# The second product of two token groups with the tokens moving instead of the weights, the gate applied to its inputs, and a dozen smaller moves

## The chip, the cores and the metric

One core of a Trainium2 chip runs the whole program. Its engines work side by side, each through its own queue in order: TensorE (PE in the profile, its weight loads PEld), VectorE (DVE), ScalarE (ACT), GpSimd (POOL) and SyncE (SP), which only issues DMAs here. The metric is device time in microseconds, the median of several runs.

## The reference, cut to what matters

```
# 4 batches, 8 heads, 576 positions, head 64: windowed attention, window 64
x = softmax(mask(q @ k.T / 8)) @ v           -> x [2304, 512]
x = elu(x @ w_in) @ w_out                    # w_in [512, 2048]
logits = x @ w_gate                          # [2304, 8]
P = exp(logits - max); 8 times: rows to sum 1, columns to sum 2304/8
out = sum over e of P[:, e] * (relu(x @ w1[e]) @ w2[e])    # 8 experts, w1[e] [512, 1024]
```

All of it is float32. Every product is made of three fp32r products (high x high, high x low, low x high), so each operand is split into a rounded high part (ScalarE) and a remainder (VectorE or GpSimd).

## The kernel before

The order of the work is written out by hand: the functions append instructions to each engine's queue in the order in which the loops at the end call them, and no scheduler reorders them.

Attention (0 to about 185 us) goes through pairs of heads: `pair_load` and `v_load` fetch q, k, v, `pair_T` transposes q and k on TensorE (L316), `grp_S`, `grp_E`, `grp_N`, `grp_P`, `grp_V` make scores, exponentials, normalisation, transposes and the product with v. `v_shift` makes a copy of v that is shifted by 64 rows. `warm` puts matmuls with zeros between. The loads stand on SP's queue.

The first feed-forward block (to about 520 us) has steps of `step_in` and `step_out` (L204 to 206, L531 to 533), four 128-wide slices of w_in at a time over five blocks of tokens (four of 512, one of 256); `elu` hands its later parts on through `run_later`.

The gate is interleaved with the last of these steps and the first expert steps: `gate_a` computes the logits of a block with the eight experts (and their low halves) on the partitions, `gate_b` turns them round with small matmuls against `sel` (L576), and `sink_parts` does the row and column normalisations on `Pr`, one piece per expert step.

The experts come in two ways. For the first 768 tokens and experts 0 to 4 they are plain (`e_in`, `e_out`, to about 866 us), while VectorE, ScalarE and GpSimd also prepare the sums of weight blocks (`p_tasks`, `q_tasks`) that the second way needs and SP stores them.

From 866 us on the second way runs: a seven-product (Winograd form of Strassen) scheme over groups g of 768 tokens, group 0 with experts 5 to 7, groups 1 and 2 with all eight. A period is one group, one expert and half of its hidden columns; there are 6 + 16 + 16 = 38 of them, each of seven steps. A step has two calls of `l1` (six matmuls each, 128x128 weights standing, 384 tokens moving, L1046) and one call of `l2` for a period that began eight steps earlier (18 matmuls, L1119: 128 tokens of the hidden layer standing, 256 columns of w2 moving). In `l1` the running sums in PSUM are copied out by ScalarE (`keep`, L1059; L1081 for `r21`) or added by VectorE (`add`, L1054; L1076), sums are made on VectorE (`ssum`, L1063), and `hid` and `hid_low` split them into high (ScalarE, L1019) and low part (VectorE L1024, GpSimd L1028). TensorE may add the next product to such a running sum only when the copy of the last one is done. `l2` adds its three 128x256 results to the accumulator `oa[g]` with the gate `Pr` as a scalar per token (VectorE, L1140; L1138 the first time), and in the last period of a group the finished quarter is stored. All groups share one accumulator buffer, so that a group's first L1138 waits for the store of the group before.

Of the kernel before, what the change touches and what calls it, by code (L numbers as in the profile page):

```python
# [18 lines left out]
def kernel(  # L19
# [14 lines left out]
    nc = tc.nc  # L34
# [30 lines left out]
    sel = const.tile([2 * E, E], F32, name="sel")  # L65
# [191 lines left out]
    def pair_load(pi):  # L257
# [3 lines left out]
        for z, (nm, src) in enumerate((("q", q), ("k", k))):  # L261
# [279 lines left out]
    def moe1_out(st, extra):  # L541
        step_out(st)
        u, j, i = st
        if u == NU - 1 and i == UF - 1:
# [7 lines left out]
            if j == len(blocks) - 2:  # L552
                extra += sink_parts()
# [4 lines left out]
    def gate_a(j):  # L558
# [7 lines left out]
        t = work.tile([P, TB], F32, tag="m", bufs=2, name="lgT")[:2 * E]  # L566
        nc.vector.tensor_copy(t[:, :n], lg[:2 * E, :n])
        lgT[j] = t

    def gate_b(j):  # L570
        t0, n = blocks[j]
        lt = ps_sm("lt")
        nt = n // P
        t = lgT.pop(j)
# [4 lines left out]
        nc.vector.tensor_copy(  # L579
            Lg[:, t0 // P:t0 // P + nt, :], lt[:, :nt * E].rearrange("p (t e) -> p t e", e=E)  # L580
        )
# [3 lines left out]
    def sink_parts():  # L585
# [35 lines left out]
        def cols():  # L621
# [3 lines left out]
            nc.vector.tensor_scalar(rc, t[:, :E], 1e-9, None, op0=ALU.add)  # L625
            nc.vector.reciprocal(rc, rc)
            nc.vector.tensor_scalar(rc, rc, float(NT) / E, None, op0=ALU.mult)
# [12 lines left out]
        return [p0, p1, first] + [mid] * 7 + [cols]  # L640
# [273 lines left out]

    P2 = {}
# [95 lines left out]

    chains = {}
# [20 lines left out]
    def l1(k, n, p, pi):  # L1033
# [17 lines left out]

        def add(nm, a):
            t = tmp("c", 5, nm)
            nc.vector.tensor_tensor(out=t, in0=o, in1=d[a], op=ALU.add)  # L1054
            d[nm] = t
# [8 lines left out]

        if pi == 1:
            keep("a")
        elif pi == 2:
            add("c11", "a")
            hid_low(*hid(key, 0, d["c11"], True))
        elif pi == 6:  # L1070
            keep("u")
        elif pi == 5:
# [3 lines left out]
            nc.vector.tensor_tensor(out=t, in0=c, in1=d["v"], op=ALU.add)  # L1076
            d["c22"] = t
            hid_low(*hid(key, 2, t, True))
        elif pi == 3:
            d["r21"] = tmp("s", 6, "r21")  # L1080
            nc.scalar.activation(d["r21"], o, AF.Relu)  # L1081
            ssum("s3", "c11", "r21", ALU.subtract)
            h3 = hid(key, 5, d["s3"], False)
            ssum("s1", "c22", "r21", ALU.add)
            ssum("s2", "c11", "s1", ALU.subtract)
            h2 = hid(key, 4, d["s2"], False)
            h1 = hid(key, 3, d["s1"], False)
            for h in (h3, h2, h1):
                hid_low(*h)
        elif pi == 4:  # L1090
            add("c21", "u")
            h1 = hid(key, 1, d["c21"], True)
            ssum("s4", "c21", "s2", ALU.add)
            hid_low(*h1)
            after.append(lambda: hid_low(*hid(key, 6, d["s4"], False)))
            del chains[key]


# [3 lines left out]
    def l2(k, x):  # L1102
        g, e, pp = periods[k]
        pi = out_order[x]
        if x == 0:
            banks.reverse()
            ot["A"] = P2["ps2"].tile([P, 1024], F32, tag=banks[0], bufs=1, name=banks[0])
            if k and periods[k - 1][0] != g:
# [6 lines left out]
        fresh = pi in (1, 7, 2)  # L1115
        for c in range(3):
# [10 lines left out]
        i, j, init = {  # L1127
            1: (0, 0, True), 7: (1, 1, True), 6: (1, 0, True), 4: (1, 0, False),
            5: (1, 1, False), 2: (0, 0, False), 3: (0, 1, True),
        }[pi]  # L1130
        last = pi in (2, 5, 4, 3)
# [9 lines left out]
        if last and e == E - 1 and pp == NP // 2 - 1:  # L1141
# [7 lines left out]
    with tc.manual_schedule():  # L1149
# [26 lines left out]
        for n in range(2):  # L1176
            pair_T(n)
            warm(2)
# [34 lines left out]
        for m in range(NST + 3):  # L1213
# [26 lines left out]
            for n in old:  # L1240
                if n > NG and n % NG == 0:
# [16 lines left out]
            for n in new:  # L1258
                if n and n % NG == 0:
# [14 lines left out]
        nc.vector.tensor_copy(sel[0:E, :], ident[0:E, 0:E])  # L1274
        nc.sync.dma_start(out=sel[E:2 * E, :], in_=ident[0:E, 0:E])
# [25 lines left out]
        for s, st in enumerate(steps):  # L1301
# [5 lines left out]
            if s:  # L1307
# [107 lines left out]
        for nm in ("w2p", "hp", "tp"):  # L1415
# [68 lines left out]
```

## Time and profile before

| | |
|---|---|
| three runs | 2008.22, 2011.4, 2015.02 us, median 2011.4 |
| profiled execution | 2014.06 us, span of its instructions 2011.6 us |
| TensorE busy | 1989.5 us, 99% of the span |
| VectorE, ScalarE, GpSimd busy | 69%, 43%, 38% |
| granted clock | mean 0.998 |

The page's engine rows count an engine as busy while an instruction of it runs, and matmuls overlap, so a busy TensorE can still lose time between two starts. The number that matters is from the start of one run of matmuls to the start of the next.

### The profile page before, as it was taken

What the parts mean: (1) busy time and instruction counts of PE and PEld (TensorE: products, weight loads), DVE (VectorE), ACT (ScalarE), POOL (GpSimd) and SP (SyncE); (2) the same over time, 40 slices, a digit from 0 to 9 for tenths busy, and PEclk for the clock granted to TensorE, in tenths of its full rate; (3) what the DMA queues carried; (4) which work ended last, traced back from release to release, by engine and by line L of the source; (5) the groups of instructions that cost most, each with busy time, mean ns of one, the idle gap of its engine ahead of it and who ended that gap; (6) DMA issues with size and microseconds to landing.
All of it is one profiled execution on the core that took longest, in us unless ns stands there. A gap on an engine that the chain in (4) does not pass through costs nothing.

```text
span 2011.6 us, 36449 instructions
## 1 busy us (share of the span) xinstructions
PE 1989.5 (99%) x13190; PEld 1844.9 (92%) x13190; DVE 1394.1 (69%) x2727; ACT 860.6 (43%) x1839; POOL 755.7 (38%) x725
## 2 busy tenths in 40 slices
PE   9999999999999999999999999999999999999998
PEld 7778888898888888889999999999999999999998
DVE  6745676767698665657776776767777767777676
ACT  8766455555443443333343333333333333333332
POOL 5323232334255555343363332332344323333332
PEclk9999999999999999999999999999999999999999
DMA  9751254458599999958878878778788788887784
GB/s 212 160 106 40 76 177 155 164 187 294 203 364 337 369 364 367 333 196 270 277 247 270 250 250 247 252 250 248 247 276 274 247 245 250 250 250 248 249 247 128
DMA packets 290866, 481.59 MB, mean 239 GB/s; under 512 B 78528, under 2 KB 145152, under 8 KB 286848
## 3 DMA queue, kind: packets, MB, share of 16 engines
q1 hardware_dynamic: 290608, 479.24, 74.7%
q8 instruction: 105, 1.72, 0.3%
q14 instruction: 73, 0.60, 0.1%
q10 hardware_dynamic: 80, 0.03, 0.0%
HBM read 348.14 MB, written 126.88 MB: 236 GB/s over the span
## 4 chain that ended last, share of the span: by engine, by line
PE 83%; DVE 5%; issue 4%; DMA 3%; ACT 3%; POOL 1%; SPq 1%; DVEq 0%; POOLq 0%; ACTq 0%
PE la L1046 15%; PE oa L1119 13%; PE ob L1119 13%; PE lb L1046 11%; PE ac L884 2%; PE ac L883 2%; PE ac L885 2%; PE p L867 2%; PE p L866 2%; PE p L865 2%; PE p L205 2%; PE p L206 2%; PE p L204 2%; PE ac L532 2%; PE ac L533 2%
## 5 line engine op out<-in xcount | busy, mean ns | idle before, releaser
L1028 POOL TENSOR_TENSOR h<-s,h 128x384 fp32r<-128x384 f32 x304 | 373.4, 1246 | 714.4 <-ACT h L1019 506.6
L1046 PE MATMUL la<-xf,w1f 128*128 128x384 f32 x1824 | 363.1, 337 | 6.8 <-ACT u L1059 6.2
L1046 PEld LDWEIGHTS la<-xf,w1f 128*128 128x128 f32 x1824 | 312.6, 189 | 9.8 <-ACT u L1059 8.6
L1119 PE MATMUL oa<-w2f,h 128*128 128x256 f32 x2394 | 307.3, 282 | 0.8 <-DVE acc L1140 0.8
L1119 PE MATMUL ob<-w2f,h 128*128 128x256 f32 x2394 | 307.2, 282 | 0.0
L1119 PEld LDWEIGHTS oa<-w2f,h 128*128 128x128 f32 x2394 | 302.0, 190 | 1.0 <-DVE acc L1140 1.0
L1119 PEld LDWEIGHTS ob<-w2f,h 128*128 128x128 f32 x2394 | 302.0, 190 | 0.0
L1024 DVE SCALAR_TENSOR_TENSOR h<-c,h 128x384 fp32r<-128x384 f32 x228 | 194.2, 852 | 129.9 <-ACT h L1019 120.9
L1046 PE MATMUL lb<-xf,w1f 128*128 128x384 f32 x1368 | 275.1, 335 | 0.2 <-DVE c L1076 0.2
L1046 PEld LDWEIGHTS lb<-xf,w1f 128*128 128x128 f32 x1368 | 237.7, 189 | 0.7 <-DVE c L1076 0.7
L1019 ACT ACTIVATE h<-s 128x384 fp32r<-128x384 f32 x304 | 150.7, 519 | 181.2 <-DVE s L1063 101.4
L1140 DVE SCALAR_TENSOR_TENSOR acc<-oa,Pr,acc 128x256 f32<-128x256 f32 x393 | 165.2, 475 | 43.1 <-PE oa L1119 43.1
L1019 ACT ACTIVATE h<-c 128x384 fp32r<-128x384 f32 x228 | 117.8, 517 | 171.7 <-DVE c L1054 113.4
L1140 DVE SCALAR_TENSOR_TENSOR acc<-ob,Pr,acc 128x256 f32<-128x256 f32 x381 | 160.2, 475 | 38.3 <-PE ob L1119 38.3
L704 POOL TENSOR_TENSOR sw<-rw 128x256 f32<-128x256 f32 x110 | 103.8, 943 | 208.5 <-DVE f L734 158.1
L246 ACT ACTIVATE hh<-p 128x512 fp32r<-128x512 f32 (+1 forms) x80 | 39.3, 491 | 196.7 <-PE p L867 196.7
L1059 ACT ACTIVATE v<-la 128x384 f32<-128x384 f32 x76 | 37.4, 492 | 198.2 <-PE la L1046 198.2
L1063 DVE SCALAR_TENSOR_TENSOR s<-c,s 128x384 f32<-128x384 f32 x152 | 98.1, 646 | 16.1 <-DVE s L1063 0.5
L865 PE MATMUL p<-xh,f 128*128 128x512 f32 (+1 forms) x320 | 108.6, 339 | 0.0
L867 PE MATMUL p<-xh,f 128*128 128x512 f32 (+1 forms) x320 | 107.6, 336 | 0.0
L866 PE MATMUL p<-xl,f 128*128 128x512 f32 (+1 forms) x320 | 107.5, 336 | 0.0
L247 DVE SCALAR_TENSOR_TENSOR hl<-p,hh 128x512 fp32r<-128x512 f32 (+1 forms) x80 | 44.3, 556 | 89.7 <-ACT hh L246 89.7
(159 smaller groups left out, 3639.6 us busy)
## 6 DMA issues: line engine op xcount, KB each, us to landing
w1f<-wdi SPq DMA_DIRECT2D x532, 256.0 KB, 3.8
w2f<-wdo SPq DMA_DIRECT2D x266, 512.0 KB, 4.1
wdo<-f SPq DMA_DIRECT2D x28, 1024.0 KB, 7.4
rw<-in_moe_w_dram SPq DMA_DIRECT2D x220, 128.0 KB, 4.4
wdi<-f SPq DMA_DIRECT2D x27, 1024.0 KB, 6.8
wdo<-f SPq DMA_DIRECT2D x28, 768.0 KB, 5.3
wdi<-f SPq DMA_DIRECT2D x27, 768.0 KB, 5.0
raw<-in_moe_w_in_dram SPq DMA_DIRECT2D x16, 512.0 KB, 4.4
```

The source lines that it names most:

```text
L247: nc.vector.scalar_tensor_tensor(gl[:, :n], p1[:, :n], 0.0, r(gh[:, :n]), op0=ALU.max, op1=ALU.subtract)
L704: nc.gpsimd.tensor_tensor(out=sw[:, o], in0=a, in1=b, op=op)
L865: nc.tensor.matmul(p1[:, :n], w[:, s, 0, cs], xh, start=(c == 0), stop=False)
L866: nc.tensor.matmul(p1[:, :n], w[:, s, 0, cs], xl, start=False, stop=False)
L867: nc.tensor.matmul(p1[:, :n], w[:, s, 1, cs], xh, start=False, stop=(c == NCC - 1))
L1019: nc.scalar.activation(h[:, 0], src, AF.Relu if relu else AF.Copy)
L1024: nc.vector.scalar_tensor_tensor(h[:, 1], src, 0.0, r(h[:, 0]), op0=ALU.max, op1=ALU.subtract)
L1028: nc.gpsimd.tensor_tensor(out=h[:, 1], in0=src, in1=r(h[:, 0]), op=ALU.subtract)
L1046: nc.tensor.matmul(o, w[:, a, c, :], x[:, b, c, :], start=first and c == 0 and z == 0, stop=last and c == 1 and z == 2, skip_group_check=True,
L1063: nc.vector.scalar_tensor_tensor(d[nm], d[a], 0.0, d[b], op0=ALU.max, op1=op)
L1119: nc.tensor.matmul(o[:, c * HB2:(c + 1) * HB2], hs[p][:, a, c * P:(c + 1) * P], w[:, p, b, :], start=fresh and c != 1 and p == 0 and z == ...
L1140: nc.vector.scalar_tensor_tensor(a, src, pe, a, op0=ALU.mult, op1=ALU.add)
```

## The change

- `l2` of groups 1 and 2 goes through a new `l2_flip`: a 128x128 piece of w2 stands and 384 tokens move, 12 matmuls in place of 18. The result has the output columns on the partitions, so the gate can no longer be a scalar per partition. Instead `scaled` multiplies c11, c22, c21 by a broadcast row of gate values (`pb`), and r21 is made with that multiplication on VectorE, where ScalarE made it before.
- `flip` writes `Pr` transposed to memory (`prd`), `pb_load` fetches it for an expert and group, repeated on all partitions.
- One VectorE addition of 128x768 drains a step (two of 128x384 for a finished quarter, a ScalarE copy for the first product), and `out_unit` transposes each finished 128x384 piece back on TensorE (three transposes, in a bank of `l1`'s tag lb), copies it on ScalarE and stores it. Group 2 takes over group 1's accumulator.
- `put` defers the splits of `l1` to `after`, which now runs behind the copies of the next `l1`. The first `l2` comes two steps earlier.
- The gate: `gate_a` transposes the logits on VectorE and adds the halves, `gate_b` brings them into place with four small DMAs; the sinkhorn pieces start one slot later, and one small VectorE instruction of each column pass goes.
- The start: k of the first pair is loaded on ScalarE's queue, four warming matmuls go, v of pair 2 is loaded and shifted one iteration earlier, and two `step_in` instead of one stand before the last block's `m0_out`.

```diff
@@ pair_load
-                nc.sync.dma_start(
+                (nc.scalar if pi == 0 and z else nc.sync).dma_start(
@@ moe1_out
-                extra += sink_parts()
+                extra += [lambda: None] + sink_parts()
@@ gate_a
-        nc.vector.tensor_copy(t[:, :n], lg[:2 * E, :n])
-        lgT[j] = t
+        nc.vector.transpose(t[:, :n], lg[:32, :n])
...
+        nc.vector.tensor_tensor(out=u..., in0=v[:, :, :, 0:E], in1=v[:, :, :, E:2 * E], op=ALU.add)
+        lgT[j] = u
@@ gate_b
-        for tt in range(nt):
-            nc.tensor.matmul(
-                lt[:, tt * E:(tt + 1) * E], t[:, tt * P:(tt + 1) * P], sel, start=True, stop=True
-            )
-        nc.vector.tensor_copy(Lg[...], lt[...])
+        for q in range(4):
+            nc.sync.dma_start(out=Lg[32 * q:32 * q + 32, t0 // P:(t0 + n) // P, :], in_=u[:, q])
@@ sink_parts
+        def flip():
...
+            nc.tensor.transpose(t[:, 0:P], f[:, 0:P], ident)
+            nc.tensor.transpose(t[:n, P:2 * P], f[:, P:], ident)
...
+            nc.sync.dma_start(out=prd[0:P], in_=st[:, 0:P])
+            nc.sync.dma_start(out=prd[P:P + n], in_=st[:n, P:2 * P])
-        return [p0, p1, first] + [mid] * 7 + [cols]
+        return [p0, p1, first] + [mid] * 7 + [cols, flip]
@@ new: pb_load
+        t = P2["pb"].tile([P, 2, TH], F32, tag="pb", bufs=2, name="pb")
+        src = prd.rearrange("(t e) p -> e t p", e=E)[e, 6 * g:6 * g + 6]
+        nc.sync.dma_start(out=t..., in_=src.partition_broadcast(P))
@@ l1
+        def scaled(t, i):
+            if g:
+                nc.vector.tensor_tensor(out=t, in0=t, in1=pb[g, e][:, i], op=ALU.mult)
+        def put(slot, nm, relu):
+            after.append(lambda: hid_low(*hid(key, slot, d[nm], relu)))
...
         elif pi == 2:
             add("c11", "a")
-            hid_low(*hid(key, 0, d["c11"], True))
+            put(0, "c11", True)
...
         elif pi == 3:
-            nc.scalar.activation(d["r21"], o, AF.Relu)
+            if g:
+                nc.vector.scalar_tensor_tensor(
+                    d["r21"], o, 0.0, pb[g, e][:, 1], op0=ALU.max, op1=ALU.mult
+                )
+            else:
+                nc.scalar.activation(d["r21"], o, AF.Relu)
@@ new: l2_flip and out_unit
+        for c in range(2):
+            for p in range(2):
+                for z, (a, b) in enumerate(((0, 0), (0, 1), (1, 0))):
+                    nc.tensor.matmul(o[:, c], w[:, p, b, c * P:(c + 1) * P], hs[p][:, a, :], ...)
+        for cs in ((0, 1), (1, 2)) if done else ((0, 2),):
...
+            if init:
+                nc.scalar.activation(a, src, AF.Copy)
+            else:
+                nc.vector.tensor_tensor(out=a, in0=src, in1=a, op=ALU.add)
+    def out_unit(g, acT, i, c):
+        o = P2["ps2"].tile([P, 512], F32, tag="lb", bufs=2, name="ot")
+        for t in range(TH // P):
+            nc.tensor.transpose(o[:, t * P:(t + 1) * P], acT[:, c, a:a + P], ident)
+        st = tmp("s", 6, "ost")
+        nc.scalar.activation(st, o[:, :TH], AF.Copy)
+        nc.sync.dma_start(out=out[...], in_=st...)
@@ l2
+            if g == 2:
+                oa[2] = oa[1]
@@ the loops
             pair_T(n)
-            warm(2)
-                    step_in(steps[0])
-                    queue.append(steps[0])
-                    run_later()
+                    for st in steps[:2]:
+                        step_in(st)
+                        queue.append(st)
+                        run_later()
+                        run_later()
...
+                    fs = list(after) if pi != 4 else []
+                    del after[:len(fs)]
                     l1(k, s * 2 + z, p, pi)
-                    if pi != 4:
-                        while after:
-                            after.pop(0)()
+                    for f in fs:
+                        f()
...
-            if s == LAG - 1:
+            if s == LAG - 3:
                 l2(0, 0)
```

## Rows read from the trace of the kernel before

**Rows 1.** The page's engine row, whole span: busy us, share, instructions.

```profile
PE 1989.5 (99%) x13190; PEld 1844.9 (92%) x13190; DVE 1394.1 (69%) x2727; ACT 860.6 (43%) x1839; POOL 755.7 (38%) x725
```

**Rows 2.** Waits of TensorE: who, for whom, us in total, times, longest.

```profile
PE la L1046 <- ACT u L1059: 6.2, 6, 2.5
...
PE pv L412 <- DMA ve<-vo: 1.9, 1, 1.9
PE p L485 <- DVE gl L235: 1.6, 2, 0.8
...
PE oa L1119 <- DVE acc L1140: 0.8, 1, 0.8
```

**Rows 3.** Chain of waits: start us, us, what.

```profile
953.34 2.08 PE la L1046 x12
955.42 2.15 PE oa L1119 x18
...
1072.29 4.57 DMA out_dram<-acc
```

**Rows 4.** Timeline of TensorE, start of the second way: start, us, instruction, idle before.

```profile
877.12 1.21 PE L1046 MATMUL lb<-xf,w1f 128*128 128x384 f32 x6
880.79 2.29 PE L1046 MATMUL la<-xf,w1f 128*128 128x384 f32 x6 [2.47 <-ACT u L1059]
...
889.68 0.52 PE L1119 MATMUL ob<-w2f,h 128*128 128x256 f32 x3
```

**Rows 5.** Timeline of ScalarE in the same stretch.

```profile
879.43 0.52 ACT L1019 ACTIVATE h<-c 128x384 fp32r<-128x384 f32 x1 [1.70 <-DVE c L1054]
...
880.27 0.47 ACT L1059 ACTIVATE u<-la 128x384 f32<-128x384 f32 x1
```

**Rows 6.** Windows: busy us (instructions) per engine; last granted clock, DMA share, GB/s.

```profile
882.00:884.00 2.00, 1.36 (x5) 0.85 (x4) 0.30 (x1) 0.49 (x1) 0.00 (x0) 0.50 0.55 211
...
1072.00:1990.00 918.00, 915.34 (x6480) 913.28 (x6479) 655.35 (x1273) 325.12 (x685) 315.46 (x254) 1.00 0.80 249
```

**Rows 7.** VectorE by line and form, whole span: count, busy us, mean ns.

```profile
L1140 DVE SCALAR_TENSOR_TENSOR acc<-oa,Pr,acc 128x256 f32<-128x256 f32 x393 | 165.2, 475 | 43.1 <-PE oa L1119 43.1
L1063 DVE SCALAR_TENSOR_TENSOR s<-c,s 128x384 f32<-128x384 f32 x152 | 98.1, 646 | 16.1 <-DVE s L1063 0.5
L1063 DVE SCALAR_TENSOR_TENSOR s<-c,r 128x384 f32<-128x384 f32 x152 | 78.0, 555 | 23.2 <-ACT r L1081 23.2
...
L1054 DVE TENSOR_TENSOR c<-lb,u 128x384 f32<-128x384 f32 x76 | 42.0, 552 | 0.0
...
L899 DVE TENSOR_TENSOR acc<-ac,acc 128x512 f32<-128x512 f32 x12 | 7.5, 677 | 0.0
...
L959 DVE TENSOR_TENSOR xb<-xb,xt 128x384 f32<-128x384 f32 x6 | 5.8, 984 | 0.0
```

**Rows 8.** Timeline of TensorE around one block's gate turn.

```profile
516.69 1.05 PE L576 MATMUL lt<-sel,lgT 16*128 16x8 f32 x8
517.67 0.50 PE L865 MATMUL p<-xh,f 128*128 128x512 f32 x1
```

**Rows 9.** Timeline of TensorE in attention, 40 to 53 us.

```profile
40.77 0.87 PE L397 MATMUL pt<-ident,sp 128*128 128x128 f32 x6
41.58 1.53 PE L348 MATMUL s<-qkT 64*64 64x128 f32 x24
...
52.26 0.33 PE L412 MATMUL pv<-pT,ve 64*64 64x64 f32 x4 [1.89 <-DMA ve<-vo]
```

**Rows 10.** Timeline of TensorE at the start.

```profile
5.79 0.55 PE L316 MATMUL ptr<-ident,kn 96*128 96x96 f32 x2 [0.23 <-DMA kn<-in_k_dram]
6.04 1.02 PE L1173 MATMUL warm<-gw 128*128 128x512 f32 x2
...
7.18 0.72 PE L1173 MATMUL warm<-gw 128*128 128x512 f32 x2
```

**Rows 11.** DMA issues: count, KB each, median us to landing.

```profile
out_dram<-acc SPq DMA_DIRECT2D x12, 384.0 KB, 3.3
```

More of the change, by code (lines that the diff above doesn't have):

```diff
@@ L64 @@
     mask = const.tile([P, P], F32, name="mask")
-    sel = const.tile([2 * E, E], F32, name="sel")
+    const.tile([P, E], F32, name="gap")
     gwr = const.tile([P, NCC, E], F32, name="gwr")
@@ L1093, in l1, with l2_flip @@
             ssum("s4", "c21", "s2", ALU.add)
-            hid_low(*h1)
-            after.append(lambda: hid_low(*hid(key, 6, d["s4"], False)))
+            put(1, "c21", True)
+            put(6, "s4", False)
             del chains[key]
+    units = []
+    def l2_flip(g, o, w, hs, fresh, i, j, init, done):
+        acT = oa[g].rearrange("p a d -> p (a d)").rearrange("p (c t) -> p c t", c=NCC)
+        o = o.rearrange("p (c n) -> p c n", c=2)[:, :, :TH]
+        for c in range(2):
+            for p in range(2):
+                for z, (a, b) in enumerate(((0, 0), (0, 1), (1, 0))):
+                    nc.tensor.matmul(
+                        o[:, c],
+                        w[:, p, b, c * P:(c + 1) * P],
+                        hs[p][:, a, :],
+                        start=fresh and p == 0 and z == 0,
+                        stop=False,
+                        skip_group_check=True,
+                    )
+        ts = slice(i * TH, (i + 1) * TH)
+        for cs in ((0, 1), (1, 2)) if done else ((0, 2),):
+            a = acT[:, 2 * j + cs[0]:2 * j + cs[1], ts]
+            src = o[:, cs[0]:cs[1]]
+            if init:
+                nc.scalar.activation(a, src, AF.Copy)
+            else:
+                nc.vector.tensor_tensor(out=a, in0=src, in1=a, op=ALU.add)
+        if done:
+            units.append([lambda c=c: out_unit(g, acT, i, 2 * j + c) for c in range(2)])
@@ L1107, in l2 @@
             ot["A"] = P2["ps2"].tile([P, 1024], F32, tag=banks[0], bufs=1, name=banks[0])
-            if k and periods[k - 1][0] != g:
+            if g == 2:
+                oa[2] = oa[1]
+            elif k and periods[k - 1][0] != g:
                 oa[g] = accp.tile([P, 6, DM], F32, tag="acc2", name="acc2")
@@ L1115, in l2 @@
         fresh = pi in (1, 7, 2)
+        i, j, init = {
+            1: (0, 0, True), 7: (1, 1, True), 6: (1, 0, True), 4: (1, 0, False),
+            5: (1, 1, False), 2: (0, 0, False), 3: (0, 1, True),
+        }[pi]
+        last = pi in (2, 5, 4, 3)
+        done = last and e == E - 1 and pp == NP // 2 - 1
+        if g:
+            l2_flip(g, o, w, hs, fresh, i, j, init and e == 0 and pp == 0, done)
+            return
         for c in range(3):
@@ L1140, in l2 @@
                 nc.vector.scalar_tensor_tensor(a, src, pe, a, op0=ALU.mult, op1=ALU.add)
-        if last and e == E - 1 and pp == NP // 2 - 1:
+        if done:
             t0 = (2 * g + i) * TH
@@ L1239 @@
                 pair_T(n)
-            for n in old:
-                if n > NG and n % NG == 0:
+            for n in mid if m == 4 else old:
+                if n > NG and n % NG == 0 and (n // NG > 2 or m == 4):
                     v_shift(n // NG)
@@ L1257 @@
             run_later()
-            for n in new:
-                if n and n % NG == 0:
+            for n in nxt if m == 2 else new:
+                if n and n % NG == 0 and (n // NG != 2 or m == 2):
                     v_load(n // NG)
@@ L1429 @@
                 after.pop(0)()
-            if s == LAG - 1:
+            fs = [f for u in units for f in u]
+            units.clear()
+            if s == LAG - 3:
                 l2(0, 0)
@@ L1436 @@
                 nw2 += 1
+            if j == 0 and k + 1 < NPD and periods[k + 1][0] and periods[k + 1][2] == 0:
+                pb_load(*periods[k + 1][:2])
             for k2 in (k, k + 1, k + 2):
@@ L1444 @@
                         close(xs["cm"])
+        for u in units:
+            for f in u:
+                f()
         close(ps2_cm)
-        for nm in ("tp", "hp", "w2p", "w1p", "xf"):
+        for nm in ("pb", "tp", "hp", "w2p", "w1p", "xf"):
             close(P2[nm + "_cm"])
```

67 lines of the change are left out of this document (43 added, 24 removed).

## The prediction

> **What bounds the kernel now.** The page's engine row comes first: TensorE is busy 1989.5 of 2011.6 us, no other engine over 69% [rows 1]. So the end moves only if TensorE gets less to issue, or stops waiting. What it issues is read from the chain of waits, in starts: in the second way a step is 12 matmuls with 384 tokens moving in 2.08 us, then 18 with 256 columns in 2.15 us [rows 3], 4.23 us together, and a period of seven steps 29.6 us. For what it waits, the list of waits is read: 6.2 us for the copies u of L1059, 1.9 us for a shifted v, 1.6 us for the last block's low parts, 0.8 us for a drain [rows 2]. The longest stands where the second way starts, and the timeline tells its price: after the six matmuls begun at 877.12, which take 1.04 us at the usual pace, five more sixes are through only at 889.68, so 11.5 us for 5.2 us of work, 6.3 us lost [rows 4]. Of these 2.47 us are the wait for u. ScalarE has u only at 880.27, behind two splits of which the first waits for VectorE [rows 5]. The windows show why the rest is lost too: after that wait the granted clock is 0.50, the 1.2 GHz level [rows 6].
>
> **The change, part by part.** The sum is made against the profiled execution, 2014.06 us, which is 2.7 us above the median of 2011.4; the end of it is shifted by that.
>
> *The flipped l2.* Groups 1 and 2 have 32 periods of seven, 224 calls. Each goes from 18 matmuls of 256 columns to 12 of 384, the same 4608 columns. `l1` issues exactly that shape, two 128-column pieces against 384 tokens, so its 2.08 us is the price: 0.07 us less a call, 15.7 us in all [rows 3]. If it saved nothing, 0; if the first matmul after a change of shape is what makes 2.15, up to that 15.7. I take 15.0.
> The Trainium skill ("TensorE: Matmul & The Clock Gate", Back-to-back issue gap) puts a warm matmul at N/2.4 + 2.5 ns. By it 18 x 109.2 becomes 12 x 162.5, 15 ns a call and 3.4 us in all. The trace disagrees: 2.15 us over 18 is 119 ns and 2.08 over 12 is 173 ns [rows 3], some 12 ns beyond the columns, not 2.5.
>
> *What VectorE gets for it.* Per period go seven times three drains at 475 ns, 10.0 us. In come seven drains of 128x768, which no row shows: from L1054 (384, 552 ns) to L899 (512, 677 ns) a column costs 0.98 ns, so 927 ns, 6.5 us; six gate multiplications, which lie between 555 and 984 ns by the nearest rows of two SBUF inputs, taken at 646, 3.9 us; two r21 at 552, 1.1 us [rows 7]. Net +1.5 us, on 655 us in 918, or 21.1 in a period of 29.6 [rows 6]: 22.6 of the new 29.1. It still fits, and the drain of a step is needed only two `l2` later, about 6.2 us after its matmuls, so I cost it at nothing. If that cover were gone, each microsecond by which a period ran over would cost 32. ScalarE gives up r21 and gains nothing in steady state.
>
> *The output turned back.* 16 pieces (two groups, two halves, four column blocks) of three transposes. Six transposes in attention start at 40.77 and are through at 41.58 [rows 9], 0.135 us each, so 48 cost 6.5 us on TensorE (5 to 8). Their bank has the tag of `l1`'s lb. At group 1's end two of four pairs come while `l1` holds the other bank, so that the second piece waits for the ScalarE copy of the first, about 0.47 us and its hand-overs: two times 0.75, 1.5 us (0 to 3). At the very end two half drains, three transposes and a copy, 0.55 x 2 + 0.4 + 0.5 = 2.0 us, replace three drains, 3 x 0.475 = 1.4 [rows 5, 7, 9]; with two more hand-overs 0.9 us more on the path, since a store follows either way (3.3 us in the median [rows 11]).
>
> *The accumulator.* Before, VectorE waited 4.57 us for a store at the change of groups [rows 3]. At the second change nothing is waited for now, since the tile is taken over and its pieces have been read by TensorE a step earlier. At the first, ScalarE waits instead, in its first-product copy, with the keeps a and v queued behind it; TensorE needs v some 4 us later. 0.7 us late (0 to 3).
>
> *The order in `l1`.* With the splits behind the next `l1`'s copies, u no longer stands behind a split that waits for VectorE. At 880 five splits may still be ahead of u, five times 0.42 us (two take from 879.43 to 880.27 [rows 5]), so some 0.5 to 0.8 us is left of the stall, and I take it that so short a wait does not bring the clock down. The second wait there is covered by the first `l2`, which now stands in it. Gain 5.5 of 6.3 us (4 to 6.2). The other five waits for u (6.2 less 2.5, 3.7 us) and the drain's 0.8 [rows 2] mostly go: 4.0 (2 to 4.7). Next late would be the splits; their slots are used two steps (8 us) or more later.
>
> *The gate.* One block's turn holds TensorE from 516.69 to 517.67 for the eight instructions of four tiles [rows 8]; the 18 tiles of five blocks make 36, 4.4 us, and the small waits before them bring it to 4.7. VectorE's transpose in place of a copy is hidden, as VectorE is not the limit there; no row shows it. The four DMAs per block enter SP's queue in front of weight loads and stores. Only the last block's landing is waited for, by the first sinkhorn reduction, which the empty slot puts one expert step later; behind it on VectorE stand the low parts that TensorE needs. A landing takes about 3.3 us [rows 11], less than that step: 0 (up to 3 lost). `flip` costs two transposes and a hand-over, 0.3 us.
>
> *Start and the last block.* The wait for k (0.23 us) and two pairs of warming matmuls (6.04 to 6.91 and 7.18 to about 7.83) stand before the first scores [rows 10], at most 1.7 us. Later ScalarE and the loads set the pace, and the shifted v of pair 4, not of pair 2, is what is late at 52.26 [rows 9], so I keep 1.0 (-2, if the clock rises later for want of warming, to 3). The second early `step_in`, twelve matmuls of 512, covers the 1.6 us of [rows 2]: 1.6 (0 to 1.8).
>
> *The loads of the gate rows.* 16 broadcasts of 384 KB in 512-byte pieces beside a DMA share of 0.80 [rows 6]. The weights are loaded six steps ahead, so 0 (up to 6 lost).
>
> **Sum.** Gains 15.0 + 5.5 + 4.0 + 4.7 + 1.6 + 1.0 = 31.8. Costs 6.5 + 1.5 + 0.9 + 0.7 + 0.3 = 9.9. Net 21.9: 1992.2 for an execution like the profiled one, 1989.5 for the median.
>
> **Rivals.**
> 1. *The flip saves nothing on TensorE.* If the pace goes by columns alone, 4608 stay 4608 and the 15.0 us go: 2004.5. For it: 119 against 173 ns is nearly a ratio of columns. Against: the same two shapes stand side by side in every step of the trace, 2.15 and 2.08 us. The skill's figure above lies between, 2001.1. 0.10.
> 2. *The waits stay.* The splits deferred from one `l1` gather in front of u after the next, the start's stall and its half clock come back, and the five others with them: 9.5 us less, 1999.0. For it: ScalarE is in order and five splits then come in one bunch. Against: a step has 4.2 us and the bunch takes 2.3. 0.13.
> 3. *The DMAs collide.* Gate rows and their small pieces delay weights at every second period, or the logits land late: 0.4 us at 16 loads and 3 us once, 1999. 0.10.
> 4. *VectorE becomes the bound (slower).* For the end to be later than before, a period must pass 29.1 + 21.9/32 = 29.8 us. Of the 21.1, 3.5 go with the drains, so the eight new operations must cost 12.2 us, over 1.5 us each. At 1.6 us each a period is 30.4, 1.3 x 32 = 42 us more, 2031. For it: GpSimd is busy beside, and L959 shows 984 ns [rows 7]. Against: 646 and 555 ns in the same stretch. 0.05.
> The Trainium skill ("SBUF — State Buffer", SBUF: two separate sides) says that a VectorE operation with two SBUF inputs and a GpSimd operation that reads SBUF hold one port in turn, the loser blocked for the whole instruction. The trace agrees in part: the same sums have means of 555 and 646 ns, not a whole GpSimd operation more.
>
> **How the numbers follow.** Forecast 0.62, with its own range 1983 to 1997 from the bounds above; the rivals as given. A measurement of this kernel tells from no change what differs by over 0.3%, 6 us: under 2005.4 is faster. The forecast, rivals 2 and 3, and most of rival 1 are: 0.91. Within 0.3% 0.04, slower 0.05. The range takes in rivals 2 and 3 and the lower bounds of the costs: 1980 to 2002.
>
> **What would show it.** In the chain, `l2` runs of groups 1 and 2 x12 at 2.08 us, a step of 4.16; right if so, and the largest step wrong if it is 2.15 or more. The granted clock at 882 stays 1.00, and the wait for u falls under 2 us in all. No L576, no L1138. VectorE busy some 78% of the last stretch; if it nears all of it, rival 4. New waits to look for: the turned-back pieces for ScalarE, the first sinkhorn reduction for a DMA, the products after a change of groups for v. It would be wrong above all if a wait recurs in every period, as one of 0.3 us costs 10.

## The result, and the profile after

The changed kernel takes 1991.36 us in the median of five runs (1989.62 to 1994.05), the kernel before 2011.4 beside it: a ratio of 0.990, 95% interval 0.9886 to 0.9915, some 20 us faster. The prediction was 1989.5, range 1980 to 2002. The profiled execution has a span of 1987.8 us against 2011.6.

The chain of waits (start us, us, what) answers to [rows 3]: the second product is now twelve matmuls in 2.08 us, and a step is 4.16 us.

```profile
1102.72 2.08 PE oa L1145 x12
1104.80 1.04 PE la L1071 x6
1105.84 1.04 PE lb L1071 x6
1106.88 2.08 PE ob L1145 x12
```

TensorE's waits (for whom, us in total, times, longest) answer to [rows 2]. The waits for u are 0.7 us where they were 6.2, and those for gl (1.6) are gone. The drain's wait (oa) has grown to 3.5 us from 0.8. New are the turned-back pieces (ot) and two waits in the stage of the gate (L531, and L897, where the kernel before has 0.7).

```profile
PE oa L1145 <- DVE acc L1160: 3.5, 2, 2.0
PE ac L897 <- DVE acc L913: 2.1, 1, 2.1
PE ot L1168 <- ACT ost L1170: 1.8, 3, 1.0
...
PE ac L531 <- DVE acc L493: 1.2, 1, 1.2
PE la L1071 <- ACT u L1091: 0.7, 2, 0.4
...
PE ot L1168 <- DVE c L1085: 0.5, 1, 0.5
```

The windows (busy us of each engine; the last three columns are granted clock, DMA share, GB/s) answer to [rows 6]. The clock is 1.00 at 882, and also from 871 to 877, which in this kernel is the stretch behind the wait for u. VectorE is busy 719 of 898 us, 80% where 71% was.

```profile
871.00:877.00 6.00, 6.00 (x40) 6.00 (x41) 4.25 (x8) 1.71 (x4) 2.42 (x2) 1.00 1.04 404
...
882.00:884.00 2.00, 2.00 (x16) 2.00 (x15) 1.61 (x2) 1.34 (x3) 1.18 (x2) 1.00 0.86 262
1072.00:1970.00 898.00, 892.37 (x5150) 890.43 (x5149) 719.11 (x1075) 304.52 (x627) 304.79 (x253) 1.00 0.81 258
```

VectorE's new groups (count, busy us, mean ns) answer to [rows 7]: the gate multiplication and the 128x768 drain cost 698 and 951 ns.

```profile
L1081 DVE TENSOR_TENSOR c<-c,pb 128x384 f32<-128x384 f32 x192 | 133.9, 698 | 6.6
L1095 DVE SCALAR_TENSOR_TENSOR s<-c,s 128x384 f32<-128x384 f32 x152 | 110.9, 730 | 13.8 <-DVE s L1095 0.5
L1160 DVE TENSOR_TENSOR acc<-oa,acc 128x768 f32<-128x768 f32 x106 | 100.8, 951 | 26.1 <-PE oa L1145 26.1
...
L1118 DVE SCALAR_TENSOR_TENSOR r<-la,pb 128x384 f32<-128x384 f32 x64 | 35.6, 556 | 12.0 <-PE la L1071 10.6 <-DMA out_dram<-ost 1.3
```

The timeline of TensorE where the second way starts answers to [rows 4]: 0.30 us of waiting for u in place of 2.47, and the first `l2` stands where the second wait was.

```profile
869.45 1.20 PE L1071 MATMUL lb<-xf,w1f 128*128 128x384 f32 x6
870.95 1.31 PE L1071 MATMUL la<-xf,w1f 128*128 128x384 f32 x6 [0.30 <-ACT u L1091]
872.11 2.31 PE L1208 MATMUL ob<-w2f,h 128*128 128x256 f32 x18
```

Where the time went is read by stage, from the starts of the same products in each profile: the first `step_in`, the first `l1`, the first `l1` of groups 1 and 2, the last `l1`, the end. The table holds all kernels (us). Equal code does not give equal numbers everywhere: up to the first `step_in` they lie up to 2.7 us apart, from there to the first `l1` 0.3 with the old gate and 2.3 with the new, in each of groups 1 and 2 before the deferral up to 2.2. With the deferral and without the flip (e1, e2) groups 1 and 2 are equal to 0.01 us.

| kernel | to first step_in | to first l1 | to group 1 | group 1 | group 2 to last l1 | after it | span |
|---|---|---|---|---|---|---|---|
| before | 211.55 | 655.15 | 168.66 | 476.55 | 473.89 | 25.80 | 2011.60 |
| after | 210.03 | 648.99 | 161.83 | 466.51 | 471.29 | 29.17 | 1987.82 |
| e1_noflip | 211.25 | 649.84 | 162.12 | 474.13 | 471.81 | 25.69 | 1994.84 |
| e2_defer | 210.31 | 655.39 | 162.34 | 474.13 | 471.81 | 25.88 | 1999.86 |
| e3_lag | 212.24 | 655.37 | 166.45 | 474.81 | 473.75 | 25.80 | 2008.42 |
| e4_gate | 212.34 | 652.75 | 167.67 | 475.33 | 472.03 | 25.60 | 2005.71 |
| e5_front | 210.34 | 655.49 | 167.70 | 476.00 | 471.81 | 25.80 | 2007.15 |
| e6_steps | 212.55 | 653.27 | 167.26 | 477.01 | 473.74 | 25.80 | 2009.62 |
| e7_noturn | 209.82 | 650.21 | 162.12 | 467.86 | 465.63 | 25.94 | 1981.57 |
| e8_best | 212.20 | 649.56 | 162.63 | 467.23 | 471.04 | 27.93 | 1990.58 |
| e9_noport | 210.75 | 650.83 | 161.87 | 467.78 | 469.33 | 29.18 | 1989.74 |
| e10_double | 209.51 | 651.03 | 161.86 | 478.71 | 475.73 | 31.99 | 2008.83 |
| e11_spread | 209.47 | 651.25 | 162.27 | 466.51 | 469.86 | 27.17 | 1986.53 |
| e12_spread_x | 210.21 | 649.15 | 161.86 | 468.33 | 469.36 | 27.17 | 1986.08 |

Group 1 is 10 us shorter, group 2 only 2.6, and the end gives 3.4 back. That is the question for the experiments: what did the flip bring, and what took it?

### The profile page after: what moved, and what is told of

It is laid out like the page before. It is cut to its first block, busy times and chain, and to the rows that moved or that the text cites. A ratio compares the mean times of both kernels' runs of the same rounds, so it can differ in the third digit from the quotient of the medians.

```text
span 1987.8 us, 33576 instructions
## 1 busy us (share of the span) xinstructions
PE 1968.5 (99%) x11856; PEld 1826.8 (92%) x11856; DVE 1460.9 (73%) x2526; ACT 848.4 (43%) x1801; POOL 745.2 (37%) x725
## 4 chain that ended last, share of the span: by engine, by line
PE 91%; DVE 3%; ACT 2%; DMA 2%; issue 1%; SPq 0%; ACTq 0%; DVEq 0%
PE la L1071 16%; PE ob L1145 12%; PE oa L1145 11%; PE lb L1071 11%; PE p L879 3%; PE p L880 3%; PE p L881 3%; PE ac L897 3%; PE ac L898 3%; PE ac L899 3%; PE oa L1208 2%; PE ob L1208 2%; PE ac L531 2%; PE ac L532 2%; PE ac L533 2%; PE p L204 2%
## 5 line engine op out<-in xcount | busy, mean ns | idle before, releaser
L1145 PE MATMUL oa<-h,w2f 128*128 128x384 f32 x1344 | 251.3, 334 | 3.5 <-DVE acc L1160 3.5
L1145 PE MATMUL ob<-h,w2f 128*128 128x384 f32 x1344 | 251.2, 334 | 0.0
L1145 PEld LDWEIGHTS oa<-h,w2f 128*128 128x128 f32 x1344 | 234.4, 188 | 4.2 <-DVE acc L1160 4.2
L1145 PEld LDWEIGHTS ob<-h,w2f 128*128 128x128 f32 x1344 | 234.4, 188 | 0.2
L1049 DVE SCALAR_TENSOR_TENSOR h<-c,h 128x384 fp32r<-128x384 f32 x228 | 161.5, 710 | 68.4 <-ACT h L1044 64.5
L1081 DVE TENSOR_TENSOR c<-c,pb 128x384 f32<-128x384 f32 x192 | 133.9, 698 | 6.6
L1160 DVE TENSOR_TENSOR acc<-oa,acc 128x768 f32<-128x768 f32 (+1 forms) x114 | 104.9, 923 | 28.9 <-PE oa L1145 28.9
L1160 DVE TENSOR_TENSOR acc<-ob,acc 128x768 f32<-128x768 f32 (+1 forms) x110 | 101.1, 923 | 28.3 <-PE ob L1145 28.3
L1091 ACT ACTIVATE a<-la 128x384 f32<-128x384 f32 x76 | 37.4, 492 | 191.2 <-PE la L1071 191.2
L246 ACT ACTIVATE hh<-p 128x512 fp32r<-128x512 f32 (+1 forms) x80 | 39.2, 491 | 186.0 <-PE p L881 186.0
L879 PE MATMUL p<-xh,f 128*128 128x512 f32 (+1 forms) x320 | 108.7, 340 | 0.0
```

The costliest lines, as they stand in the source:

```text
L879: nc.tensor.matmul(p1[:, :n], w[:, s, 0, cs], xh, start=(c == 0), stop=False)
L1049: nc.vector.scalar_tensor_tensor(h[:, 1], src, 0.0, r(h[:, 0]), op0=ALU.max, op1=ALU.subtract)
L1081: nc.vector.tensor_tensor(out=t, in0=t, in1=pb[g, e][:, i], op=ALU.mult)
L1091: nc.scalar.activation(d[nm], o, AF.Copy)
L1145: nc.tensor.matmul(o[:, c], w[:, p, b, c * P:(c + 1) * P], hs[p][:, a, :], start=fresh and p == 0 and z == 0, stop=False, skip_group_check ...
L1160: nc.vector.tensor_tensor(out=a, in0=src, in1=a, op=ALU.add)
```

## The experiments

Differences are against the kernel before timed beside it, worked out from the ratio; the interval is worked out from that of the ratio. The kernel before has medians from 2011.4 to 2013.61 us at the four times at which it was run, so two changed kernels that ran at different times are compared by their medians and by their ratios, and where these disagree both are given.

**The change without the flip.**

```diff
-            if g:                      # scaled, r21, l2: the branches of the flip
+            if False:
-        return [p0, p1, first] + [mid] * 7 + [cols, flip]
+        return [p0, p1, first] + [mid] * 7 + [cols]
```

> The kernel after with the second products of groups 1 and 2 left in the old form (hidden values stationary, gate in the drain, no gate multiplications, no output turned back); every other edit stays. Theory: the flip gives 224 x 0.07 = 15.7 us back and takes some 10 (48 transposes, waits for ScalarE's copies, the last drain), so it nets 4 to 6: 1995.5 us (1993.5 to 1999), that is 16 of the 20 us come from the edits around it. Rival: the flip carries most of the gain (its 15 us, with turning hidden): 2004 or more. Second rival: the flip costs more than it brings: under 1991.

1995.46 us, ratio 0.9906 (0.9892 to 0.992): 18.9 us of the gain are there without the flip. The flip adds 4.1 between the medians and 1.2 between the ratios, whose intervals overlap, so the times alone do not show that it gains. The stages do: with the flip group 1 is 7.6 us shorter, group 2 only 0.5, the end 3.5 longer, 4.6 net. The rival of 2004 is out by the times, that of under 1991 by the stages.

**The order in `l1` alone, and the earlier first `l2` alone.** Both on the kernel before.

```diff
@@ e2: l1, each split
-            hid_low(*hid(key, 0, d["c11"], True))
+            put(0, "c11", True)
@@ e2: the loop
+                    fs = list(after) if pi != 4 else []
+                    del after[:len(fs)]
                     l1(k, s * 2 + z, p, pi)
+                    for f in fs:
+                        f()
@@ e3
-            if s == LAG - 1:
+            if s == LAG - 3:
```

> The kernel before with one edit: the splits of the hidden values are issued behind the next first product (nothing else). Theory: the start stall with its half clock goes (5 to 6.5 us) and the waits for u (some 4): 2001.5 us (1999.5 to 2004), and the trace shows clock 1.00 at 880 to 890. Rival: the earlier first l2 cures the start stall, the deferral only the waits for u: 2007 (2005.5 to 2008.5), with the half clock at 880 to 890 still there.

> The kernel before with one edit: the first second product is issued two steps earlier. Theory (the deferral cures the start stall): 2011 (2009 to 2013), the wait is moved and stays. Rival (the earlier l2 fills the gap): 2005.5 (2004 to 2007) and no half clock at 880 to 890.

The deferral: 2001.96 us, ratio 0.9943 (0.9932 to 0.9955), 11.5 us off (9 to 14). It is the largest part of the net gain: 6.3 us at the start by the table, 2.4 and 2.1 in groups 1 and 2 (little more there than equal code differs by; but the waits for u are 0.3 us, not 6.2). About 1 of the 6.3 belongs to the one profiled execution of the kernel before: e4, e5 and e6 have the same stall with a shorter stretch at half the clock, and against them the start is 4.9 to 5.4 us shorter. The clock at 882 with the deferral alone (windows):

```profile
882.00:884.00 2.00, 2.00 (x14) 2.00 (x13) 1.90 (x5) 0.91 (x3) 0.00 (x0) 1.00 1.03 412
```

The earlier `l2`: 2011.62 us, ratio 0.9993 (0.9985 to 1.0001), no difference that is shown. But my theory had one thing wrong: it held that only the deferral touches the start. The wait for u stays, and the six matmuls behind it take 1.31 us, not the 2.29 of [rows 4]. That is not the edit's doing: in e4 to e6, which have the old order, they take 1.32 to 1.34, and the clock falls only behind the second wait, for v, of 0.64 us. In e3 the `l2` stands in that second wait, no half clock follows, and the stage is 0.8 to 1.3 us shorter than theirs, 2.2 shorter than in the kernel before. This is one profiled execution, of mean granted clock 1.000; the other eleven have 0.997 to 1.000, so that it goes so each time is not shown. With the deferral there is nothing left for it to cure.

```profile
881.70 1.31 PE L1046 MATMUL la<-xf,w1f 128*128 128x384 f32 x6 [2.46 <-ACT u L1059]
882.86 2.31 PE L1119 MATMUL ob<-w2f,h 128*128 128x256 f32 x18
```

**The gate alone.** On the kernel before, `gate_a` and `gate_b` as changed and the empty slot ahead of the Sinkhorn parts:

```diff
-        nc.vector.tensor_copy(t[:, :n], lg[:2 * E, :n])
+        nc.vector.transpose(t[:, :n], lg[:32, :n])
...
+            nc.sync.dma_start(out=Lg[...], in_=u[:, q])
...
+                extra += [lambda: None] + sink_parts()
```

> The kernel before with one edit: the gate's logits turned on VectorE and carried by DMA instead of by TensorE, the first Sinkhorn part one slot later. Theory: 4.4 us off the stage from 212 to 867 us: 2007 (2005.5 to 2008.5). Rival: the four DMAs land late behind the weight stream and the first reduction waits: 2011 or more, with a wait for a DMA ahead of the first reduction.

2010.4 us, ratio 0.9989 (0.9981 to 0.9998): 2.2 us off, and 2.4 by its stage. It lies between theory and rival, and the mechanism of neither holds. The 36 matmuls are gone, but two waits have come, 3.9 us together, where the kernel before has 0.7:

```profile
PE ac L884 <- DVE acc L900: 2.1, 1, 2.1
...
PE ac L531 <- DVE acc L493: 1.8, 1, 1.8
```

All nine kernels with the new gate have them (1.2 to 3.0 us at L531, 2.1 at L897's place), the five without it have none at L531 and 0.6 to 0.7 at the other. None is put down to a DMA: here both are for VectorE, in three of the nine the second is for ScalarE (hh, L246).

The traces show that it is not the gate's own instructions that make VectorE late. Ahead of both waits VectorE splits the sums of weight blocks (f), and ScalarE gives it f late: the first time it waits for a store of f, the second time for GpSimd's sums (sw), in the kernel before as long as here (ScalarE's timeline, first before, then the gate alone):

```profile
492.81 1.06 ACT L729 ACTIVATE f<-rw 128x1024 fp32r<-128x1024 f32 x1 [5.74 <-DMA wdo<-f]
...
559.95 1.06 ACT L729 ACTIVATE f<-sw 128x1024 fp32r<-128x1024 f32 x1 [4.14 <-POOL sw L704]
```

```profile
493.93 1.06 ACT L730 ACTIVATE f<-rw 128x1024 fp32r<-128x1024 f32 x1 [5.57 <-DMA wdo<-f]
...
558.43 1.06 ACT L730 ACTIVATE f<-sw 128x1024 fp32r<-128x1024 f32 x1 [4.15 <-POOL sw L705]
```

From the split behind the first of them to the drain of L493 VectorE takes 11.6 us before and 11.5 here. TensorE, rid of its turns, is ready for L531 2.1 us earlier against that chain: 1.1 us after the drain's start before, 1.0 ahead of it here. So part of what was taken off TensorE comes back as waiting. Whether another of the gate's edits adds to it was not tried.

**The start alone, and the second early `step_in` alone.**

```diff
@@ e5 (with v_load and v_shift of pair 2 one iteration earlier)
-                nc.sync.dma_start(
+                (nc.scalar if pi == 0 and z else nc.sync).dma_start(
             pair_T(n)
-            warm(2)
@@ e6
-                    step_in(steps[0])
-                    queue.append(steps[0])
-                    run_later()
+                    for st in steps[:2]:
+                        step_in(st)
+                        queue.append(st)
+                        run_later()
+                        run_later()
```

> The kernel before with one edit: the front (the first k loads on ScalarE's queue, no warm-up products between the first transposes, the loads of v's second pair and their shift earlier). Theory: first scores 0.8 us earlier and the wait for v of pair 2 gone: 1.5 us off (1.0 to 2.5), first step_in earlier by that. Rival: the start is given back at the first wait for k: no difference.

> The kernel before with one edit: the second step_in issued before the last out-parts of the first unit. Theory: the stage from 212 to 867 us is shorter by the part of its 6.15 us that the gate alone did not bring (it brought 2.4): 3.5 us off (2 to 4.5), the waits of L485 for gl near 214 and 218 us gone. Rival: the waits only move behind the next drain: under 1 us off.

The start: 2009.06 us, ratio 0.9983 (0.9973 to 0.9993), 3.4 us off (1.4 to 5.4); its profile has the first scores at 7.04 us, not 7.83, and the first `step_in` 1.2 us earlier. As kernels with the same front end it anywhere from 209.5 to 212.2, the 1.2 is not resolved. The wait for the shifted v, 1.9 us before, is 0.4; but it is 0.5 in e2, which has nothing of this edit. The `step_in`: 2011.61 us, ratio 0.9991 (0.9981 to 1.0001), 1.8 us off; its stage is 1.9 us shorter and the wait of L485 for gl is gone. The theory's mechanism is right, its 3.5 was too much: 1.9 and the gate's 2.4 make 4.3, where the kernels with both are 3.9 to 6.2 below before in that stage.

One more wait of that stage is gone in all eight kernels that have every edit there, and 1.6 to 2.1 us long in the six others: that of the column sums of the sinkhorn pieces, here in the kernel before.

```profile
PE csum L623 <- DVE cs L619: 2.0, 2, 1.5
```

The one VectorE instruction less in each column pass is the edit that bears on it. No experiment made it by itself, so that it is the cause is likely, not shown.

**The output not turned back.**

```diff
-        o = P2["ps2"].tile([P, 512], F32, tag="lb", bufs=2, name="ot")
-        for t in range(TH // P):
-            nc.tensor.transpose(...)
-        st = tmp("s", 6, "ost")
-        nc.scalar.activation(st, o[:, :TH], AF.Copy)
...
-            in_=st.rearrange("p (t d) -> p t d", d=P),
+            in_=acT[:, c, i * TH:(i + 1) * TH].rearrange("p (t d) -> p t d", d=P),
```

> The kernel after without turning the output back: the 48 transposes, their 16 copies on ScalarE and their PSUM tiles are left out, the accumulator is stored as it lies (so the output lies differently). Theory: 6.5 us of TensorE, 2 to 3 us of waits for the copies, 1 us at the end: 1982 us (1980.5 to 1984). Rival: turning hides in waits that are there anyway: 1988 or more.

1983.05 us, ratio 0.9852 (0.9839 to 0.9866) against the change's 0.990: turning back costs 8.3 us between the medians, 9.7 between the ratios. In the table group 2, in whose first periods group 1's output is turned, is 5.7 us shorter and the end 3.2, group 1 is 1.4 longer: 7.5. The waits of the pieces are gone, the drain's are not:

```profile
PE oa L1145 <- DVE acc L1160: 3.5, 2, 2.0
```

So without turning, the flip is worth 12.4 us over the kernel without it (1995.46 less 1983.05), 10.9 by the ratios and 12.2 by the stages; with the 2.7 us by which these waits pass the 0.8 of the kernel without the flip, 13.6 to 15.1; 224 calls at 0.07 make 15.7. The periods tell it most directly: from its first `l1` to that of the next, a steady one takes 29.63 us without the flip and 29.12 in the change (27 of 32), and 0.51 by 32 is 16.3.

**VectorE's room.** Each gate multiplication twice:

```diff
-                nc.vector.tensor_tensor(out=t, in0=t, in1=pb[g, e][:, i], op=ALU.mult)
+                for _ in range(2):
+                    nc.vector.tensor_tensor(out=t, in0=t, in1=pb[g, e][:, i], op=ALU.mult)
```

> The kernel after with every gate multiplication on VectorE done twice (the values are then scaled by the gate squared). Six more operations of some 0.7 us in a period put VectorE from 22.6 to some 26.8 of 29.12 us. Theory: VectorE has room in the steady periods, the period stays at 29.1 us, and only the bursts ahead of the drains (1493, 1514 to 1531, 1963) grow: 1995 us (1992.5 to 1999). Rival (the one of the prediction in which VectorE is the bound): the drains come late in each period, 1 us of wait or more in each of 32: 2023 or more.

2009.61 us, ratio 0.9987 (0.9978 to 0.9995): 18 us slower than the change, between theory and rival. One period in the windows, in the order no flip, change, doubled; the fourth number is VectorE's:

```profile
1140.00:1169.12 29.12, 29.12 (x208) 29.12 (x208) 19.97 (x41) 9.89 (x22) 9.13 (x8) 1.00 0.80 250
```

```profile
1140.00:1169.12 29.12, 29.12 (x170) 29.12 (x169) 23.24 (x36) 9.64 (x21) 9.45 (x8) 1.00 0.81 253
```

```profile
1140.00:1169.12 29.12, 29.12 (x170) 29.12 (x169) 27.27 (x42) 9.59 (x20) 9.84 (x8) 1.00 0.79 253
```

The flip adds 3.3 us of VectorE to this window (2.9 to a period, which is 29.63 us without it), and a further 4 cost nothing there: the same 170 matmuls in the same 29.12 us, in 26 of the 32 periods. The price is paid where VectorE carries more or has less time: 3.7 us at the first change of groups, 12.6 at the second, 2.8 at the end. The waits are these:

```profile
PE oa L1146 <- DVE acc L1161: 5.6, 2, 3.4
PE la L1071 <- ACT v L1092: 4.8, 3, 2.8
PE la L1071 <- ACT u L1092: 3.5, 4, 1.5
```

They are not the whole price. Beside the drain's waits of 2.2 and 3.4 us the granted clock falls to 0.50, the 1.2 GHz level, which it does at neither place in the change. At the second change of groups (windows):

```profile
1510.10:1516.90 6.80, 6.06 (x19) 6.06 (x20) 6.73 (x8) 2.83 (x5) 3.88 (x3) 0.50 0.21 57
```

**GpSimd beside VectorE.** In the change the drain of 1493 is late after three sums on VectorE that stretched while GpSimd made the low halves of the next group's inputs. First VectorE, then GpSimd (start us, us):

```profile
1485.25 0.54 DVE L1118 SCALAR_TENSOR_TENSOR r<-la,pb 128x384 f32<-128x384 f32 x1
1485.83 3.73 DVE L1095 SCALAR_TENSOR_TENSOR s<-c,r 128x384 f32<-128x384 f32 x2
1489.66 1.41 DVE L1095 SCALAR_TENSOR_TENSOR s<-c,s 128x384 f32<-128x384 f32 x1
```

```profile
1484.87 2.16 POOL L970 TENSOR_TENSOR xf<-xb,xf 128x768 fp32r<-128x768 f32 x1
1486.98 2.16 POOL L970 TENSOR_TENSOR xf<-xt,xf 128x768 fp32r<-128x768 f32 x1
```

The experiment takes GpSimd out:

```diff
-        nc.gpsimd.tensor_tensor(out=t[:, 1], in0=src, in1=r(t[:, 0]), op=ALU.subtract)
+        nc.scalar.activation(t[:, 1], src, AF.Copy)
```

> The kernel after with the low halves of the regrouped inputs (seven 128x768 subtractions on GpSimd, 2.1 us each, ahead of each group) replaced by copies on ScalarE, so their values are left out. Theory: the 128x384 operations on VectorE with two operands in SBUF took 1.4 to 2.2 us near 1486 to 1493 because GpSimd worked beside them; without it they take 0.55 to 0.75 us, the 1.6 us wait at 1493 goes: 1989.8 us (1988.8 to 1990.8). Rival: the wait belongs to ScalarE's order (the copies of the splits late), and more copies on ScalarE make it longer: 1992 or more.

1988.31 us, ratio 0.9882 (0.9866 to 0.9898). The same three sums, with GpSimd idle there:

```profile
1489.32 0.55 DVE L1118 SCALAR_TENSOR_TENSOR r<-la,pb 128x384 f32<-128x384 f32 x1
1489.91 1.03 DVE L1095 SCALAR_TENSOR_TENSOR s<-c,r 128x384 f32<-128x384 f32 x2
1491.04 0.56 DVE L1095 SCALAR_TENSOR_TENSOR s<-c,s 128x384 f32<-128x384 f32 x1
```

The two take 1.03 us where they took 3.73, and the wait at 1493 is gone, as the theory said. The time is not settled by it: groups 1 and 2 together are only 0.7 us shorter (937.1 against 937.8), as two periods ahead of the change of groups are longer by 1.3 us in all, and the ratio's interval overlaps the change's. The Trainium skill ("SBUF — State Buffer", SBUF: two separate sides) says that a VectorE operation with two SBUF inputs and a GpSimd operation that reads SBUF lock a shared port for a whole instruction. The stretched sums agree with that here: 2.7 us more for two, against GpSimd's 2.16 each; the r21 beside it, whose one input is in PSUM, keeps 0.54.

**Can the lost time be had back?** Three tries on the change.

```diff
@@ all three, in the last period: c21, s4 and their splits go to a list (e11, e12: as two)
+            if k == NPD - 1 and p == 1:
+                late.append(tail)
@@ e8: run behind the l2 of the same step; first piece of a unit behind the step's first l1
+                    if z == 0 and us:
+                        us.pop(0)()
@@ e11: run one by one, two and three steps later; first piece ahead of the step's l2
+            if fs and k < NPD:
+                fs.pop(0)()
+            if late and s >= NPD * 7 + 1:
+                late.pop(0)()
@@ e12: e11, and in x_form
-        nc.gpsimd.tensor_tensor(out=t[:, 1], in0=src, in1=r(t[:, 0]), op=ALU.subtract)
+        nc.vector.tensor_tensor(out=t[:, 1], in0=src, in1=r(t[:, 0]), op=ALU.subtract)
```

> The kernel after with two edits: in the last period the work on VectorE that follows the last first product (c21, its gate multiplication, s4 and their splits) is issued behind the second product of that step, and the two pieces of a turned-back quarter are issued apart, the first behind the step's first l1, the second behind its l2. Theory: the 2.0 us wait at 1963 goes and 2 of the 2.6 us of waits between 1514 and 1531: 1987.5 us (1986 to 1989.5). Rival: the waits are put elsewhere (the burst on VectorE is only late by a step, the piece put ahead of l2 waits for its drain): 1991.

> The kernel after with two edits: in the last period c21 and s4 with their splits are issued two and three steps later, behind second products that nothing else follows on VectorE; of a turned-back quarter the first piece is issued ahead of the step's second product (behind both l1), the second behind it. Theory: the wait of 2.0 us at 1963 goes whole, and 2 of the 2.6 us of waits of the turned-back pieces at 1514 to 1531: 1987.5 us (1986 to 1989.3). Rival: as in the first try, the piece ahead of the second product waits for VectorE's drain instead: 1989.5 or more.

> The kernel with the spread work and pieces, and the low halves of the regrouped inputs on VectorE instead of GpSimd (same values). Theory: GpSimd no longer works beside VectorE's operations there, seven operations of some 1 us are added to VectorE, the wait at 1493 goes: 1.5 us below the kernel with the spread alone, 1986 us (1984.5 to 1988). Rival: the added operations are themselves the burst ahead of the drain: no gain on the kernel with the spread alone.

e8: 1992.12 us, ratio 0.9897 (0.9881 to 0.9912), no gain: the rival. At the end 1.2 us come back, but the piece put ahead waits for its drain:

```profile
PE ot L1175 <- DVE acc L1167: 2.0, 2, 1.7
```

e11: 1989.44 us, ratio 0.9889 (0.9876 to 0.9903). The wait of 2.0 us at the last `l1` is gone whole (the end is 27.17 us, 2.0 less) and those of the pieces are 1.5, not 2.3; the drain at 1493 still keeps TensorE 1.2:

```profile
PE oa L1157 <- DVE acc L1172: 1.2, 1, 1.2
...
PE ot L1180 <- DVE acc L1172: 0.7, 1, 0.7
PE ot L1180 <- DVE c L1085: 0.5, 1, 0.5
...
PE ot L1180 <- ACT ost L1182: 0.3, 1, 0.3
```

e12: 1988.65 us, ratio 0.9886 (0.9873 to 0.99). The drain's wait is gone, but the operations added to VectorE make the first piece wait 1.6 us, so the rival holds: no gain on e11.

```profile
PE ot L1180 <- DVE acc L1172: 1.6, 1, 1.6
```

By the stages the spread is worth 3.4 us on the change (groups 1 and 2 1.4, end 2.0); by the times 2 to 3, with intervals that overlap. It is likely, not shown, to beat the change.

## Why the prediction was right

The measured median lies 1.9 us above the forecast. By its steps:

- *The flipped l2* (15.0): right. The step is 4.16 us, and 13.6 to 15.1 is what the runs leave for it, 16.3 the periods. Rival 1 falls with the x12 in 2.08 us.
- *The output turned back* (6.5 + 1.5 + 0.9): right, 8.3 to 9.7 timed, 7.5 by stage.
- *The order in `l1`* (5.5 + 4.0): right, 11.5 (9 to 14) timed, 10.8 by stage. Rival 2, the splits gathering before u, is out: 0.30 us is left of 2.47. That the first `l2` stands in the second wait was right too, and in e3's profiled execution this alone keeps the clock up.
- *VectorE* (+1.5 a period at no cost): the flip puts 2.9 into a period: a gate multiplication costs 698 ns where 646 was taken, a drain 951 for 927, and the sums beside them grew to 730 from 646. The steady part of the argument held all the same. What failed is that the drain's 0.8 would mostly go. The drain's waits grew to 3.5 us. At the last `l1` the cover of 6.2 us is gone, since no `l1` stands between the next second products, and the burst ahead of the drain is longer by the multiplications. At 1493 the cover stands, but VectorE is late by more: the drain of the product begun at 1485.28 starts at 1494.34, behind the sums that stretched beside GpSimd. Of rival 4 this is all that came.
- *The gate* (4.7): the step that failed most. It counted each microsecond taken off TensorE as one off the time, with VectorE "not the limit there". By itself it brought 2.2 to 2.4, as TensorE ran into the chain of weight sums on ScalarE and VectorE, and 3.9 us of waits took the place of 0.7. The transpose on VectorE, which the prediction called hidden, is not what it waits for. Rival 3's wait of a reduction for the logits did not come.
- *The second step_in* (1.6): 1.8 to 1.9. *The start* (1.0): 3.4 (1.4 to 5.4) timed, 1.2 by stage; whether it was sized too low is open. The wait for the column sums (2.0), which is gone too, had no term.
- *The accumulator* (0.7): no wait for its store shows. *The loads of the gate rows* (0): no wait shows in a steady period.

By the stages of the two profiled executions the forecast is closer than by its terms: 1.5, 6.2, 6.8 and 9.3 us are gained up to the first `step_in`, from there to the first `l1`, to group 1 and to the end, where the terms make 1.0, 6.0, 5.5 and 9.4. That is in part luck, as errors of both signs met. The gate alone brought 2.3 too little and the drains cost 2.7 more; on the other side stand the column sums' 2.0, the order's 1.3 to 2.0 and what the start brought beyond its 1.0. And these stages make 23.8 us, because the profiled execution of the kernel before is slower than its median and that of the change is the fastest of its five; the medians lie 20.0 apart.

## What to carry to other kernels

A term that is paid by instruction count (0.07 us by 224 calls) can be read from a neighbouring row of the same shape; in group 1 it came true to 0.2 us, 7.6 for 7.8. Work taken off the engine that is busy 99% of the time comes off the time only as far as no other chain runs close behind it: look for the slack of that chain at the place, not at the shares of the page. The cover that hides an edit in the steady state has to be costed again at each place where it is missing or the other engine has more to do: changes of groups, the last period, the store. When a change bundles several edits, time the plain reorderings first: here a change of issue order alone was worth more than the rewritten product, which cost the most and netted 1 to 5 us.

## What the runs showed of the hardware

The granted clock did not follow from the length of a wait. In seven of the nine kernels with the new gate it fell to 0.50, the 1.2 GHz level, at one of the two new waits, in none at both. At L531 it fell in five (e1, e7, e9, e10, e11), with waits of 1.84 to 2.96 us, and stayed up in the other four, with 1.20 to 2.92. The stretches after 1.84 us in the kernel without the flip and after 2.92 us in e8 (windows, the clock before the last two columns):

```profile
505.40:508.40 3.00, 3.00 (x8) 2.31 (x7) 2.73 (x4) 0.24 (x1) 0.98 (x2) 0.50 1.10 390
```

```profile
506.20:509.20 3.00, 3.00 (x13) 2.48 (x14) 3.00 (x5) 0.14 (x1) 2.17 (x4) 1.00 1.11 386
```

At L897 the wait is 2.1 us in all nine, and the clock fell in two, the change and e12. The change, and then the kernel without the flip:

```profile
557.00:560.60 3.60, 3.60 (x10) 2.11 (x10) 3.60 (x8) 1.06 (x1) 1.45 (x3) 0.54 1.06 372
```

```profile
560.20:563.80 3.60, 3.32 (x14) 2.27 (x15) 3.60 (x7) 1.38 (x2) 1.71 (x3) 1.00 1.06 376
```

In the same 3.0 us run 8 matmuls in the one and 13 in the other, in the same 3.6 us 10 and 14. The stage up to the first `l1` goes with it: 649.8 to 651.3 us in the five whose clock fell at L531, 649.0 to 649.6 in the three others with all its edits.

At the start of the second way 2.47 us and then 0.64 us of waiting brought the 1.2 GHz level in all four profiled kernels that have both; 2.46 us alone, with the first `l2` behind it, did not, nor did 0.30 and then 0.64 in e2. What such a wait costs beyond itself is not to be read from its length. The clock shows in the times of equal code: of the 56 executions of the kernel before beside the experiments the four with a mean granted clock of 1.000 take 2008.0 to 2010.7 us, the 16 with 0.997 take 2011.8 to 2018.0.
